# Emitting tile transposes one by one between the matmuls of a product, with two more idle products at the start

## The chip, the core and the metric

The kernel runs on one NeuronCore of a Trainium2 chip. A core has a matrix engine (TensorE, "PE" in the profile, with its weight loads shown apart as "PEld"), a vector engine (VectorE, "DVE"), a scalar engine (ScalarE, "ACT"), GpSimd ("POOL") and SyncE ("SP"), which here issues the DMAs. Each engine works through its own instructions in the order in which they were emitted; semaphores order the engines among each other. Matmuls read SBUF and write PSUM; ScalarE and VectorE read PSUM and write SBUF.

The metric is the device time of one execution in microseconds (us), the median of several runs.

## What is computed

One layer over 2048 positions of width 640, in float32, with no bias:

```
xn = layernorm(x)                                  # x: 2048 x 640
q, k, v = split(xn @ wqkv)                         # 32 heads of 20
s = softmax(q . k[pos - 2*w], w = 0..7) @ v[...]   # 8 keys, every second position back
s = s @ wo
h = (xn @ w_gate) * (xn @ w_up)                    # 640 -> 1536
g = silu(h @ w_down)                               # 1536 -> 640
out = x + s * g
```

All large products must keep float32's accuracy. The kernel gets it from the faster 32-bit matmul format fp32r: an operand is split into a high part (rounded by a ScalarE copy) and a low part (the rest, by a subtraction), and a product is the sum of high x high, high x low and low x high.

## The kernel before, in words

The 2048 positions are 16 tiles of 128. Everything is emitted by hand in one order (the tile framework is in its manual mode), so the order of the program text is the order on each engine.

- `mm3` (line 82) is a product: for KD = 5 slices of the inner dimension and three pairs of parts it emits 15 matmuls into one PSUM tile. `qkv(u, i)` (218) is one such product of 300 or 360 columns, followed by two ScalarE copies out of PSUM (226, 227). `gate_up(f, ch)` (312) is two of 512 columns (gate, then up), with ScalarE, VectorE or GpSimd taking the results. `out_proj(s)` (397) is two of 320 columns, each followed by a ScalarE copy (404).
- A tile must have its inner dimension on the partitions, so each tile is transposed on TensorE: five transposes of 128 x 128 against an identity matrix. `transposed` (191) does it: four go into one PSUM tile and one into a second, both of tag "q"; after each PSUM tile ScalarE copies out the high part (196) and VectorE subtracts for the low part (197). `trans(s)` (199) does it for an input tile, `trans_o(s)` (386) for a tile of the attention's output.
- PSUM tag "q" has four buffers. `qkv`, `out_proj`, the idle products and the transposes all take theirs from it. A buffer is free again when the engines that read it are done.
- `norm` (176) normalises tiles on VectorE, with one square root on ScalarE in its midst; `norm(12, 4)` works on the last four input tiles.

The head of the program (lines 556 to 607) is a list of calls: norms, weight splits, `trans(0)` to `trans(15)`, and the first `qkv` and `gate_up` products between them. TensorE's first work is a loop of three idle products against the identity (146), whose result nobody reads. In this list `trans(6)` stands between the two products of `gate_up(1, 0)` and `trans(11)` between those of `gate_up(1, 1)` (the argument `amid`); the others stand between whole calls.

Then, to about 556 us, the attention of 12 units runs on VectorE in portions (`advance`) while TensorE does the remaining `qkv` and `gate_up` products. At the end the attention's output comes back tile by tile (`load_o`, into buffers "wraw", "hs" and "t"), and a loop over s (678) calls `trans_o(s + 1)`, then `sum_wd` (VectorE sums of the down weights), then `out_proj(s)`, then `split_wd`. The last stage, after 645 us, is the down product in seven sub-products a pair of tiles, and the gating.

Of the kernel before, what the change touches and what calls it, by code (L numbers as in the profile page):

```python
# [11 lines left out]
F32 = mybir.dt.float32  # L12
F32R = mybir.dt.float32r
AF = mybir.ActivationFunctionType
# [5 lines left out]
P = 128  # L20
# [27 lines left out]
def kernel(  # L48
# [9 lines left out]
    nc = tc.nc  # L58
# [10 lines left out]
    def st(shape, tag, bufs, dt=F32):  # L69
        cnt[0] += 1  # L70
        return sb.tile(shape, dt, tag=tag, bufs=bufs, name=f"{tag}_{cnt[0]}")

    def pt(shape, tag, bufs):
        cnt[0] += 1
        return ps.tile(shape, F32, tag=tag, bufs=bufs, name=f"{tag}_{cnt[0]}")

    def split(eng, raw, hi, lo):

        nc.scalar.activation(hi, raw, AF.Copy)  # L79
        eng.tensor_sub(lo, raw, hi.bitcast(F32))  # L80

    def mm3(acc, pairs, first=True, last=True):

        pairs = list(pairs)
        runs = [(a[i], b[j]) for i, j in ((0, 0), (0, 1), (1, 0)) for a, b in pairs]
        for n, (a, b) in enumerate(runs):
            nc.tensor.matmul(acc, a, b, start=first and n == 0, stop=last and n == len(runs) - 1)  # L87


    wq_raw, wq = {}, {}  # L90

    def load_wq(g, parts):
        c3 = 3 * GROUPS[g] * DH
        wq_raw[g] = []
        for p in parts:
            t = st([P, p[-1] - p[0], c3], "wraw", 3)
            for k0, k1 in zip(p, p[1:]):
                nc.sync.dma_start(t[:, k0 - p[0]:k1 - p[0]], wqkv[g][:, k0:k1, :])
                wq_raw[g].append((k0, k1, t[:, k0 - p[0]:k1 - p[0]]))

    def split_wq(g, eng, ks=(0, KD)):
        c3 = 3 * GROUPS[g] * DH
        if g not in wq:
            wq[g] = st([P, KD, c3], "wqh", 1, F32R), st([P, KD, c3], "wql", 1, F32R)
        for k0, k1, t in wq_raw[g]:
            if ks[0] <= k0 < ks[1]:
                split(eng, t, wq[g][0][:, k0:k1], wq[g][1][:, k0:k1])
# [16 lines left out]
    def load_x(s, n, t, cuts=(0, D)):  # L124
        j = tile_column(s)
        for c0, c1 in zip(cuts, cuts[1:]):
            nc.sync.dma_start(t[:, :, c0:c1], xv[:, j:j + DIL * (n - 1) + 1:DIL, c0:c1])  # L127
        for i in range(n):
            xt[s + i] = t[:, i, :]
# [13 lines left out]
    load_x(15, 1, xb[:, 2:3])  # L143
    ident = st([P, P], "ident", 1)
    make_identity(nc, ident)
    for _ in range(3):
        nc.tensor.matmul(pt([P, 3, P], "q", 4), ident, ident.unsqueeze(1).to_broadcast([P, 3, P]), start=True,
                         stop=True)
    eps_t = st([P, 1], "eps", 1)
    nc.vector.memset(eps_t, EPS)  # L150

# [6 lines left out]
    def xT_tile(s):  # L158
        if s % TPC == 0:
            y = st([P, 2, KD, CH], "xc", NCH, F32R)  # L160
            xT.append((y[:, 0], y[:, 1]))
        hi, lo = xT[s // TPC]
        c = (s % TPC) * P
        return hi[:, :, c:c + P], lo[:, :, c:c + P]
# [24 lines left out]
                                    op0=ALU.subtract, op1=ALU.mult)  # L189

    def transposed(src, hi, lo):
        for k0, k1 in ((0, 4), (4, KD)):
            p = pt([P, k1 - k0, P], "q", 4)
            for k in range(k0, k1):
                nc.tensor.transpose(p[:, k - k0, :], src[:, k * P:(k + 1) * P], ident)  # L195
            nc.scalar.activation(hi[:, k0:k1, :], p, AF.Copy)  # L196
            nc.vector.tensor_sub(lo[:, k0:k1, :], p, hi[:, k0:k1, :].bitcast(F32))  # L197

    def trans(s):
        transposed(xt[s], *xT_tile(s))  # L200


    UN = [(g, r) for g in range(len(GROUPS)) for r in range(DIL)]
# [14 lines left out]
    def qkv(u, i):  # L218
        g, r = UN[u]
        c = GROUPS[g] * DH  # L220
        p = pt([P, 3 * c], "q", 4)
        hi, lo = xT[(r * NE + i) // TPC]
        t0 = (i % TPC) * P
        a, b = (hi[:, :, t0:t0 + P], lo[:, :, t0:t0 + P]), wq[g]
        mm3(p, [([t[:, k, :] for t in a], [t[:, k, :] for t in b]) for k in range(KD)])
        nc.scalar.activation(kv_t[u][:, :, W - 1 + i, :], p[:, c:].rearrange("p (a c) -> p a c", a=2), AF.Copy)  # L226
        nc.scalar.activation(q_t[u][:, i, :], p[:, :c], AF.Copy)
        for i0, i1 in ((1, 5), (5, NE)):
            if i == i1 - 1:
                for p0, p1 in ((0, 112), (112, 127)):  # L230
                    nc.sync.dma_start(kv_t[u][p0 + 1:p1 + 1, :, i0 - 1:i1 - 1, :],
                                      kv_t[u][p0:p1, :, W - 1 + i0:W - 1 + i1, :])
# [63 lines left out]
    def advance(budget):  # L296
        credit[0] += budget
        while running and credit[0] > 0:
            try:
                credit[0] -= next(running[0][1])  # L300
            except StopIteration:
                running.pop(0)
        if not running:
            credit[0] = 0
# [4 lines left out]
    def gate_up_half(f, ch, n, p, c=slice(0, CH)):  # L309
        mm3(p[:, c], [([t[:, k, n, :] for t in wf[f]], [t[:, k, c] for t in xT[ch]]) for k in range(KD)])  # L310

    def gate_up(f, ch, between=(), amid=(), part=None):
        if part is None:
            pp = [pt([P, CH], "g", 2), pt([P, CH], "u", 2)]
            c = slice(0, CH)
        else:
            pp, c = part, slice(CH // 2, CH)
        gate_up_half(f, ch, 0, pp[0], c)
        for act in amid:
            act()  # L320
        gs = st([P, CH], "gs", 2)
        nc.scalar.activation(gs, pp[0], AF.Copy)  # L322
        for act in between:
            act()
        share = (c.stop - c.start) / CH
        finish_piece()
        advance(PACE * 3.25 * share)
        gate_up_half(f, ch, 1, pp[1], c)

        def finish():  # L330
            hs = st([P, CH], "hs", 2)
            if running:
                nc.vector.tensor_mul(hs, pp[1], gs)  # L333
            else:
                nc.scalar.activation(hs, pp[1], AF.Copy)
                nc.gpsimd.tensor_mul(hs, hs, gs)  # L336
            nc.sync.dma_start(h_scr[ch * TPC:(ch + 1) * TPC, :, f, :].rearrange("t p c -> p t c"),
                              hs.rearrange("p (t c) -> p t c", c=P))

        unfinished.append(finish)  # L340
        if not running:
            finish_piece()
        advance(PACE * 3.25 * share)
# [3 lines left out]
    def finish_piece():  # L347

        while unfinished:
            unfinished.pop(0)()  # L350
# [37 lines left out]
    def trans_o(s):  # L388
        if s == NT - 2:
            oT[s] = st([P, KD, P], "hs", 2, F32R), st([P, KD, P], "hs", 2, F32R)  # L390
        else:
            tag, n = ("kv", 2) if s == 0 else ("wf", 4) if s < NT - 2 else ("t", 2)
            y = st([P, 2, KD, P], tag, n, F32R)
            oT[s] = y[:, 0], y[:, 1]
        transposed(o_t.pop(s), *oT[s])

    def out_proj(s):
        a = oT.pop(s)
        y = st([P, D], "gs", 2)
        for n in range(2):  # L400
            c = slice(n * HALF, (n + 1) * HALF)
            p = pt([P, HALF], "q", 4)
            mm3(p, [([t[:, k, :] for t in a], [t[:, c] for t in wo_s[k]]) for k in range(KD)])
            nc.scalar.activation(y[:, c], p, AF.Copy)
        nc.sync.dma_start(s_scr[s], y)
# [87 lines left out]
    bank, kept, g_t, sx_t = {}, {}, {}, {}  # L493
# [63 lines left out]
    mv1 = moments(1, 1)  # L557
    split_wq(0, nc.gpsimd, (0, 3))
    trans(0)
    split_wq(0, nc.gpsimd, (3, KD))  # L560
    load_x(13, 1, xa[:, 0:1])
    norm(1, 1, mv1)
    begin_unit(0)
    mv2 = moments(2, 2)
    qkv(0, 0)
    trans(1)
    split_wf(0, nc.gpsimd, range(KD + 1))
    norm(2, 2, mv2)
    qkv(0, 1)
    split_wf(1, nc.gpsimd, range(KD + 1))  # L570
    part0 = gate_up_first(0, 0)
    trans(2)
    trans(3)
    mask = st([1, NE, W], "mask", 1)
# [6 lines left out]
    gate_up(0, 0, part=part0)  # L581
    trans(4)
    trans(5)
    gate_up(1, 0, amid=(lambda: trans(6),))
    trans(7)
    norm(8, 4)
    load_wf(2)
    qkv(0, 4)
    qkv(0, 5)
    gate_up(0, 1)  # L590
    trans(8)
    qkv(0, 6)
    trans(9)
    norm(12, 4)
    qkv(0, 7)
    trans(10)
    gate_up(1, 1, amid=(lambda: trans(11),))
    begin_unit(1)
    for i in range(8):
        if i == 3:  # L600
            running.append((0, attention(0)))
        if i == 2:
            load_wq(1, ((0, 3), (3, 5)))
        qkv(1, i)
        if i < 4:
            trans(12 + i)
        advance(PACE * 1.9)
    running.append((1, attention(1)))
    split_wq(1, nc.gpsimd)
# [68 lines left out]
    for s in range(NT):  # L678
        k, part = divmod(s - 1, 2)
# [27 lines left out]
    for m in range(n_prod):  # L707
        n, j = divmod(m, 7)
# [52 lines left out]
```

## Time and profile before

| what | value |
|---|---|
| median of 3 runs | 803.85 us (803.69 to 804.44) |
| the profiled execution's own time | 803.25 us |
| its span, first to last instruction | 801.5 us |
| TensorE busy | 791.7 us, 99% |
| VectorE busy | 635.2 us, 79% |
| ScalarE busy | 236.7 us, 30% |
| GpSimd busy | 137.7 us, 17% |
| transposes (line 195) | 160: 80 of input tiles, 80 of attention tiles |

Rows of the profile name a line of the kernel, an engine, an operation and the tiles, "out<-in". A row of the view in order of time begins with the start and the length in us and ends with the number of instructions merged into it ("x5") and, in brackets, the idle time of the engine ahead of it and what ended that. Matmuls are pipelined and their ends are modelled, so the step from one start to the next tells more than a length; TensorE counts as busy while it merely holds a pipelined matmul. In the view of stretches each row gives, after the length, every engine's busy time, then the granted clock of TensorE (1.00 is full), the share of the DMA engines and GB/s.

### The profile page before, as it was taken

To read this page: it belongs to the slowest core of one execution; us is meant where nothing else is said; L and a number is where in the kernel's file an instruction comes from. 1 tells how busy PE (TensorE), PEld (TensorE's weight loads), DVE (VectorE), ACT (ScalarE), POOL (GpSimd) and SP (SyncE) were. 2 spreads that over 40 slices of the span, in tenths; PEclk is the share of its full clock that TensorE was granted. 3 is DMA by queue.
4 is the path that set the end of the run, shared out by engine and by line. 5 is a ranking of instruction groups with operands and counts; after the bars stand their busy time and mean duration, and the time that the engine had idled before them with its cause. 6 is when DMAs were issued, how large, how long until landed. Compare 5 with 4: busy or idle time off the path is not lost.

```text
span 801.5 us, 11434 instructions
## 1 busy us (share of the span) xinstructions
PE 791.7 (99%) x4564; PEld 721.5 (90%) x4564; DVE 635.2 (79%) x638; ACT 236.7 (30%) x560; POOL 137.7 (17%) x109
## 2 busy tenths in 40 slices
PE   8999999999999999999999999999999999999997
PEld 6889898898898898898989889888899999999997
DVE  7676899999999979997999999990144457878775
ACT  4323212121112111211121112102355554444442
POOL 5201210122012100500231001104266500000000
PEclk9999999999999999999999999999999999999999
DMA  9122012141122221313141222422867464565523
GB/s 318 63 80 89 28 61 79 51 121 48 49 88 86 87 70 60 116 39 97 49 137 42 68 72 78 129 61 75 214 191 206 139 251 136 201 224 185 178 99 132
DMA packets 68413, 90.07 MB, mean 112 GB/s; under 512 B 16952, under 2 KB 48776, under 8 KB 68360
## 3 DMA queue, kind: packets, MB, share of 16 engines
q1 hardware_dynamic: 68360, 89.34, 34.7%
q8 instruction: 36, 0.59, 0.3%
q14 instruction: 17, 0.14, 0.1%
HBM read 51.90 MB, written 28.31 MB: 100 GB/s over the span
## 4 chain that ended last, share of the span: by engine, by line
PE 96%; DMA 1%; POOL 1%; issue 1%; ACT 0%; DVE 0%; SPq 0%; POOLq 0%
PE q L87 35%; PE g L87 20%; PE u L87 20%; PE q L526 10%; PE u L526 5%; PE g L526 3%; PE q L195 2%; DMA wraw<-in_wqkv 1%; DMA hs<-o_scr 0%; POOL wf L80 0%; POOL wql L80 0%; ACT xc L196 0%; DVE q L512 0%; POOL hs L336 0%; SPq L127 0%
## 5 line engine op out<-in xcount | busy, mean ns | idle before, releaser
L87 PE MATMUL g<-xc,wf 128*128 128x512 f32 (+1 forms) x735 | 176.3, 391 | 0.1
L87 PE MATMUL u<-xc,wf 128*128 128x512 f32 (+1 forms) x735 | 176.1, 390 | 0.0
L87 PEld LDWEIGHTS u<-xc,wf 128*128 128x128 f32 x735 | 135.6, 187 | 32.2
L87 PE MATMUL q<-wqh,xc 128*128 128x300 f32 (+1 forms) x960 | 161.8, 311 | 2.1 <-ACT xc L196 1.6
L87 PEld LDWEIGHTS g<-xc,wf 128*128 128x128 f32 x735 | 135.2, 188 | 31.2 <-POOL wf L80 0.3
L87 PEld LDWEIGHTS q<-wqh,xc 128*128 128x128 f32 x960 | 146.8, 189 | 4.2 <-ACT xc L196 2.1
L258 DVE TENSOR_TENSOR t<-q,kv 128x1600 f32<-128x1600 f32 (+1 forms) x48 | 101.7, 2119 | 9.1 <-DMA kv<-kv 9.1
L279 DVE TENSOR_TENSOR t<-e,kv 128x1600 f32<-128x1600 f32 (+1 forms) x48 | 97.6, 2053 | 1.1
L261 DVE TENSOR_REDUCE lg<-t 128x80 f32<-128x1600 f32 (+1 forms) x48 | 92.6, 1930 | 1.2
L322 ACT ACTIVATE gs<-g 128x512 f32<-128x512 f32 x48 | 28.8, 599 | 207.5 <-PE g L87 198.8
L80 POOL TENSOR_TENSOR wf<-wraw,wf 128x256 fp32r<-128x256 f32 (+2 forms) x22 | 44.8, 2053 | 249.1 <-ACT wf L79 249.1
L87 PE MATMUL q<-wql,xc 128*128 128x300 f32 (+1 forms) x480 | 87.0, 311 | 0.2 <-POOL wql L80 0.2
L287 DVE TENSOR_TENSOR t<-t,t 128x1600 f32<-128x1600 f32 (+1 forms) x36 | 78.0, 2166 | 1.1
L226 ACT ACTIVATE kv<-q 128x200 f32<-128x200 f32 (+1 forms) x96 | 33.4, 348 | 145.9 <-PE q L87 145.9
L87 PEld LDWEIGHTS q<-wql,xc 128*128 128x128 f32 x480 | 74.8, 189 | 0.6 <-POOL wql L80 0.5
L526 PE MATMUL q<-xc,wf 128*128 128x320 f32 x432 | 67.3, 309 | 0.0
L526 PEld LDWEIGHTS q<-xc,wf 128*128 128x128 f32 x432 | 64.3, 188 | 0.0
L80 POOL TENSOR_TENSOR wql<-wraw,wqh 128x300 fp32r<-128x300 f32 (+4 forms) x15 | 33.4, 2254 | 147.8 <-ACT wqh L79 147.8
L197 DVE TENSOR_TENSOR wf<-q,wf 128x512 fp32r<-128x512 f32 (+1 forms) x26 | 11.5, 486 | 41.7 <-ACT wf L196 41.7
L87 PE MATMUL q<-wf,wf 128*128 128x320 f32 x156 | 36.8, 317 | 0.0
L197 DVE TENSOR_TENSOR xc<-q,xc 128x512 fp32r<-128x512 f32 (+1 forms) x32 | 13.9, 484 | 20.7 <-ACT xc L196 20.7
L333 DVE TENSOR_TENSOR hs<-u,gs 128x512 f32<-128x512 f32 x39 | 26.6, 683 | 0.8 <-issue 0.8
(144 smaller groups left out, 900.9 us busy)
## 6 DMA issues: line engine op xcount, KB each, us to landing
h_scr<-hs SPq DMA_DIRECT2D x48, 256.0 KB, 2.3
wraw<-in_wgu SPq DMA_DIRECT2D x12, 640.0 KB, 4.5
t<-h_scr SPq DMA_DIRECT2D x8, 768.0 KB, 7.4
s_scr<-gs SPq DMA_DIRECT2D x16, 320.0 KB, 2.3
hs<-s_scr SPq DMA_DIRECT2D x16, 320.0 KB, 3.7
gs<-in_x SPq DMA_DIRECT2D x16, 320.0 KB, 4.2
out<-q SPq DMA_DIRECT2D x15, 320.0 KB, 2.4
wraw<-h_scr SPq DMA_DIRECT2D x12, 384.0 KB, 6.1
```

Source lines behind the costliest of these rows:

```text
L80: eng.tensor_sub(lo, raw, hi.bitcast(F32))
L87: nc.tensor.matmul(acc, a, b, start=first and n == 0, stop=last and n == len(runs) - 1)
L195: nc.tensor.transpose(p[:, k - k0, :], src[:, k * P:(k + 1) * P], ident)
L197: nc.vector.tensor_sub(lo[:, k0:k1, :], p, hi[:, k0:k1, :].bitcast(F32))
L226: nc.scalar.activation(kv_t[u][:, :, W - 1 + i, :], p[:, c:].rearrange("p (a c) -> p a c", a=2), AF.Copy)
L258: nc.vector.tensor_mul(t, q.rearrange("p i c -> p (i c)").unsqueeze(1).to_broadcast([P, 2, NE * c]), places(0, j))
L261: nc.vector.tensor_reduce(out=lg[:, :, j:j + 2].rearrange("p n a -> p a n"), in_=heads(t), op=ALU.add, axis=AX.X)
L279: nc.vector.tensor_mul(heads(t), pw, heads(places(1, j)))
L287: nc.vector.tensor_add(acc, acc, t)
L322: nc.scalar.activation(gs, pp[0], AF.Copy)
L333: nc.vector.tensor_mul(hs, pp[1], gs)
L526: nc.tensor.matmul(p, y[:, i, k], wd_t[name][k][:, l], start=new and r == 0, stop=r == len(runs) - 1, skip_group_check=True)
```

## The change

Transposes are no longer emitted where `trans` or `trans_o` is called. They are put into a list, `single`, as five small functions a tile, and `mm3` emits one of them after every second matmul (seven places in a product of 15). The PSUM tile is taken, and the ScalarE copy and the VectorE subtraction are emitted, when the first and the last transpose of their bank are emitted. A call of `trans(s)` without `mixed` still empties the list at once; so does `trans_o(0)`. Input tiles 0 to 5 and attention tile 0 therefore stay in groups; input tiles 6 to 15 and attention tiles 1 to 15 go between matmuls: 6 and 7 in `gate_up(1, 0)`, 8 in `qkv(0, 6)`, 9 in `qkv(0, 7)`, 10 and 11 in `gate_up(1, 1)`, 12 to 15 in `qkv(1, 0)` to `qkv(1, 3)`, attention tile s + 1 in the first half of `out_proj(s)`. The call of `norm(12, 4)` stays between `trans(9)` and `qkv(0, 7)`.

The idle product becomes a function; four are emitted at the start in place of three, and one more after `trans(0)`.

```
--- before.py
+++ after.py
@@ mm3
         for n, (a, b) in enumerate(runs):
             nc.tensor.matmul(acc, a, b, start=first and n == 0, stop=last and n == len(runs) - 1)
+            if n % 2 and single:
+                single.pop(0)()
+
+    single = []
+
+    def singles():
+        while single:
+            single.pop(0)()
@@ head
-    for _ in range(3):
+    def idle_product():
+
         nc.tensor.matmul(pt([P, 3, P], "q", 4), ident, ident.unsqueeze(1).to_broadcast([P, 3, P]), start=True,
                          stop=True)
+
+    for _ in range(4):
+        idle_product()
@@ transposed
     def transposed(src, hi, lo):
+
+        bank = {}
+
+        def one(k, k0, k1):
+            if k == k0:
+                bank[k0] = pt([P, k1 - k0, P], "q", 4)
+            p = bank[k0]
+            nc.tensor.transpose(p[:, k - k0, :], src[:, k * P:(k + 1) * P], ident)
+            if k == k1 - 1:
+                nc.scalar.activation(hi[:, k0:k1, :], p, AF.Copy)
+                nc.vector.tensor_sub(lo[:, k0:k1, :], p, hi[:, k0:k1, :].bitcast(F32))
+
         for k0, k1 in ((0, 4), (4, KD)):
-            p = pt([P, k1 - k0, P], "q", 4)
             for k in range(k0, k1):
-                nc.tensor.transpose(p[:, k - k0, :], src[:, k * P:(k + 1) * P], ident)
-            nc.scalar.activation(hi[:, k0:k1, :], p, AF.Copy)
-            nc.vector.tensor_sub(lo[:, k0:k1, :], p, hi[:, k0:k1, :].bitcast(F32))
-
-    def trans(s):
+                single.append(lambda k=k, k0=k0, k1=k1: one(k, k0, k1))
+
+    def trans(s, mixed=False):
         transposed(xt[s], *xT_tile(s))
+        if not mixed:
+            singles()
@@ trans_o
         transposed(o_t.pop(s), *oT[s])
+        if s == 0:
+            singles()
@@ the list of calls
     trans(0)
+    idle_product()
...
     trans(4)
     trans(5)
-    gate_up(1, 0, amid=(lambda: trans(6),))
-    trans(7)
+    trans(6, True)
+    trans(7, True)
+    gate_up(1, 0)
     norm(8, 4)
     load_wf(2)
     qkv(0, 4)
     qkv(0, 5)
     gate_up(0, 1)
-    trans(8)
+    trans(8, True)
     qkv(0, 6)
-    trans(9)
+    trans(9, True)
     norm(12, 4)
     qkv(0, 7)
-    trans(10)
-    gate_up(1, 1, amid=(lambda: trans(11),))
+    trans(10, True)
+    trans(11, True)
+    gate_up(1, 1)
...
     for i in range(8):
...
+        if i < 4:
+            trans(12 + i, True)
         qkv(1, i)
-        if i < 4:
-            trans(12 + i)
         advance(PACE * 1.9)
```

## The prediction

> **What bounds the kernel now.** I read the page first (span, busy shares), then busy time by stretch, then what TensorE waits for, then the groups of instructions, and last the order of time around each place that the change touches.
>
> ```profile
> span 801.5 us, 11434 instructions
> PE 791.7 (99%) x4564; PEld 721.5 (90%) x4564; DVE 635.2 (79%) x638; ACT 236.7 (30%) x560; POOL 137.7 (17%) x109
> 75.00:556.00 481.00, 481.00 (x2520) 422.72 (x2519) 440.76 (x305) 95.91 (x250) 72.83 (x27) 1.00 0.24 74
> PE q L87 <- ACT xc L196: 1.6, 2, 1.1
> PE q L195 <- DVE t L188: 0.7, 1, 0.7
> PE q L195 <- DMA hs<-o_scr: 0.4, 1, 0.4
> ```
>
> TensorE (PE) is busy 791.7 of 801.5 us, and between 75 and 556 us all 481.00 of 481.00 us (the columns are the length of the stretch, then PE and PE's weight loads). So PE's own queue is the path: whatever is added to it, or makes it wait, before 645 us is paid in full, and nothing later takes it up. The waits that the profile lists for PE are short and lie in the head and at one tile of the attention output. No listed wait belongs to tiles 4 to 15 of the input. So emitting their transposes elsewhere can only gain if a transpose itself gets cheaper.
>
> **Part 1: what a transpose costs in a group and alone.** Each tile has five transposes, L195. These rows are the chain that ended last (start, length, what; x15 products of 512 columns among it), the durations of one line (minimum, median, maximum in ns) and PE in order of time:
>
> ```profile
> 595.37 4.42 PE q L87 x30
> 599.79 0.55 PE q L195 x5
> 600.34 4.42 PE q L87 x30
> 544.01 3.50 PE u L87 x15
> L195 PE MATMUL q<-ident,xc x40: 270/272/273, 29.5 to 59.6; 128*128 128x128 f32 x40
> 27.79 1.92 PE L87 MATMUL u<-xc,wf 128*128 128x256 f32 x15
> 29.54 1.25 PE L195 MATMUL q<-ident,xc 128*128 128x128 f32 x10
> ```
>
> A group of five takes 0.55 us, 0.110 each. Ten in a row last 1.25 us from the first start to the last end, and one lasts 0.272 us, so the step from transpose to transpose is (1.25 - 0.27) / 9 = 0.109 us. Four such steps leave 0.55 - 0.436 = 0.114 us for the step from the last transpose to the next product. A transpose that stands alone between two matmuls has only that second kind of step; the matmul ahead of it keeps its own pace. Alone it therefore costs 0.114 against 0.110 in the group. Fifty transposes in the head (tiles 6 to 15) and 75 at the end (attention tiles 1 to 15) are moved: 125 x 0.005 = **+0.6 us**. Ends: 0, if the step is the same, and 125 x 0.009 = +1.1, if the last step is 0.118; below nothing stands the rival "hidden transposes".
>
> **Part 2: tile 6 in gate_up(1, 0).** The transposes write PSUM tiles of tag "q", of which there are four; a tile takes two, and each is free only after ScalarE (L196) and then VectorE (L197) have read it.
>
> ```profile
> 30.55 3.74 PE L87 MATMUL g<-xc,wf 128*128 128x512 f32 x15
> 30.86 1.68 DVE L197 TENSOR_TENSOR xc<-q,xc 128x512 fp32r<-128x512 f32 x4 [0.45 <-ACT xc L196]
> L197 DVE TENSOR_TENSOR xc<-q,xc x32: 278/460/693, 8.1 to 75.0; 128x512 fp32r<-128x512 f32 x16, 128x128 fp32r<-128x128 f32 x16
> ```
>
> Tiles 4 and 5 are still transposed at once and fill all four. Before, tile 6 came after 15 gate matmuls; now its first transpose comes after two. Fifteen take 3.50 us, 0.233 each, and the first really follows the group of ten, at 29.54 + 10 x 0.110 = 30.64 (the row's 30.55 is its early start). So tile 6 is reached at about 30.64 + 0.47 = 31.1 us, while VectorE finishes the first of the four subtractions, a long one of 0.69, at 30.86 + 0.69 = 31.55. Nothing else of PE can pass: **+0.5 us** (0.3 to 0.6).
>
> **Part 3: tiles 8 to 11 and norm(12, 4). This is the largest term.** Before, tile 9's evictions were emitted ahead of norm(12, 4). Now tile 9's transposes, and with them its ScalarE copies and VectorE subtractions, are emitted inside qkv(0, 7), behind norm(12, 4); VectorE works in that order.
>
> ```profile
> 49.84 0.71 PE L195 MATMUL q<-ident,xc 128*128 128x128 f32 x5
> 51.16 0.89 DVE L197 TENSOR_TENSOR xc<-q,xc 128x512 fp32r<-128x512 f32 x2 [3.16 <-ACT xc L196]
> 52.46 0.71 PE L195 MATMUL q<-ident,xc 128*128 128x128 f32 x5
> 52.66 0.34 ACT L226 ACTIVATE kv<-q 128x200 f32<-128x200 f32 x1 [1.36 <-PE q L87]
> 55.08 0.71 PE L195 MATMUL q<-ident,xc 128*128 128x128 f32 x5
> 53.73 0.89 DVE L197 TENSOR_TENSOR xc<-q,xc 128x512 fp32r<-128x512 f32 x2 [1.68 <-ACT xc L196]
> 54.54 0.87 DVE L172 BATCH_NORM_STATS2 stats<-o 128x6 f32<-128x320 f32 x2
> 58.66 0.30 ACT L180 ACTIVATE rstd<-mv,eps 128x4 f32<-128x4 f32 x1 [4.80 <-DVE mv L173]
> 62.10 1.68 DVE L197 TENSOR_TENSOR xc<-q,xc 128x512 fp32r<-128x512 f32 x4
> ```
>
> The reader sees norm(12, 4) hold VectorE from 54.54 until the next subtraction at 62.10, 7.56 us, and ScalarE stand at its square root (L180) for 4.80 us. Call the start of qkv(0, 6) zero (49.84 before). 52.46 to 55.08 is one tile and one qkv: 2.62 us, 15 matmuls at 0.138 and a group. In the changed order tile 8's fourth transpose starts after 8 matmuls and 3 transposes, at 1.45. By the rows (fourth transpose at 49.84 + 3 x 0.109 = 50.17, subtractions from 51.16 to 52.05, the next work 0.81 after such a start: as tile 9's at 53.73 and 54.54) its VectorE work is over near 1.45 + 0.99 + 0.81 = 3.25, call it 3.2, and norm(12, 4) runs from 3.2 to 10.76. Tile 9's first subtraction ends at 10.76 + 0.69 = 11.45. PE meanwhile would reach the third transpose group as follows: two qkv with five single transposes each, 2 x 2.64 = 5.28, then twelve gate matmuls and five transposes, 12 x 0.233 + 5 x 0.112 = 3.36, which is tile 11's first transpose at 8.65. By then all four PSUM tiles are taken: two by tile 9, two by tile 10, none of them subtracted. It waits for tile 9's first, to about 11.5: **+2.85 us**. On the way it may already lose part of this (0.2 to 0.4 at tile 9, which needs tile 8's PSUM; 0.5 at tile 10's second group, since qkv(0, 7)'s result waits behind the square root on ScalarE), but the end at 11.5 is set by VectorE, so these are in the 2.85. Ends: 2.3 if VectorE is ready 0.5 earlier, 3.4 if tile 10's second group takes the late tile. Behind the waiting transpose stands the rest of PE's program.
>
> **Part 4: tiles 12 to 15 in qkv(1, 0) to (1, 3).** Same PSUM tag: qkv's result and two transposed banks of one tile, then the next qkv's result, four in all. The next tile's first transpose comes two matmuls into the next qkv, 2.64 + 0.28 = 2.92 after the start of the one before; the first bank is released at 1.45 + 0.99 + 0.69 = 3.13 (0.99 from its fourth transpose to its subtraction, as in part 3), or, if the bank of the qkv result is taken, at about 3.3: its first copy starts at 52.66, 2.82 after zero, lasts 0.34, and a second follows. That is 0.2 to 0.4 a tile, three times: **+0.9 us** (0.4 to 1.2). No attention work is on VectorE yet.
>
> **Part 5: attention tile 1.** Here the old order waits.
>
> ```profile
> 599.63 0.71 PE L195 MATMUL q<-ident,t 128*128 128x128 f32 x5
> 565.46 3.67 PE L87 MATMUL u<-xc,wf 128*128 128x512 f32 x15
> 569.49 1.01 PE L195 MATMUL q<-ident,hs 128*128 128x128 f32 x5 [0.36 <-DMA hs<-o_scr]
> 570.50 4.42 PE q L87 x30
> ```
>
> PE is free at 565.46 + 15 x 0.233 = 568.96, starts the tile at 569.49 as its load lands in pieces, and the products follow at 570.50 rather than 568.96 + 0.70 = 569.66 (0.70 is from 599.63, where an undisturbed group starts, to 600.34 in part 1). That is 0.84 late. Now two products go first (0.29), the first transpose waits about 0.24 and the others find their pieces: **-0.6 us** (-0.8 to -0.3).
>
> The other tiles of that stage are covered: transposes end ten matmuls into out_proj(s), and the result is read 20 matmuls x 0.147 = 2.9 us later, low half 10 matmuls later still. What moves ahead of their subtraction on VectorE is sum_wd:
>
> ```profile
> 587.33 0.89 DVE L197 TENSOR_TENSOR wf<-q,wf 128x512 fp32r<-128x512 f32 x2 [3.19 <-ACT wf L196]
> 588.13 0.57 DVE L435 TENSOR_TENSOR lg<-wraw 128x320 f32<-128x320 f32 x1
> 588.80 1.00 DVE L436 TENSOR_TENSOR lg<-wraw,lg 128x320 f32<-128x320 f32 x1
> ```
>
> Even if its 1.67 us lie wholly ahead, the subtraction ends near 589.9, and the low half is read from about 591.2. Without that cover each tile would cost the overshoot. SyncE's loads into the "t" buffer (s = 3, 6, 9) now wait for a transpose about 2 us later, with out_proj's stores and the weight loads behind them; tile 8 is wanted four periods of 4.97 us later, so this costs nothing.
>
> **Part 6: the head.** Start and length on PE and the row of VectorE that tile 1 waits for, then two stretches (length, PE busy, weight loads, DVE, ACT, POOL, granted clock):
>
> ```profile
> 1.37 4.21 PE L147 MATMUL q<-ident 128*128 128x384 f32 x6 [1.37 <-POOL ident masks.py:199]
> 6.28 0.76 PE L195 MATMUL q<-ident,t 128*128 128x128 f32 x5 [0.70 <-DVE t L188]
> 8.10 1.26 PE L87 MATMUL q<-wqh,xc 128*128 128x300 f32 x5 [1.06 <-ACT xc L196]
> 10.95 1.12 DVE L188 TENSOR_SCALAR t<-t,mv,rstd 128x640 f32<-128x640 f32 x1
> 12.23 0.92 PE L195 MATMUL q<-ident,t 128*128 128x128 f32 x5
> 5.83:9.24 3.41, 1.90 (x11) 1.44 (x12) 2.47 (x8) 2.88 (x8) 2.70 (x4) 1.00 1.03 374
> 9.25:12.66 3.41, 3.25 (x14) 2.79 (x13) 3.24 (x8) 0.19 (x1) 2.46 (x3) 0.50 0.94 312
> ```
>
> PE was busy 1.90 of the first stretch and got half the clock in the next. An idle product is two instructions of about 0.64 us; the fourth starts near 5.4, gets the full clock from 5.83 and ends near 6.28, where tile 0 starts: nothing, or +0.4 at half clock. The fifth fits between 7.0 and 8.10. With the clock kept, tile 1, which cannot start before 10.95 + 1.12 = 12.07, ends 0.3 earlier (five transposes last 0.71 at full clock, 0.92 here, and start 0.16 sooner), and ScalarE, POOL and PE behind it follow: **-0.3 us**. Ends: -0.4, and +1.0 if the now thinner stretch from 9.25 loses the clock for the next.
>
> **Sum.** 0.6 + 0.5 + 2.85 + 0.9 - 0.6 - 0.3 = +3.95 us on the profiled execution's 803.25 us, 807.2; it stands 0.6 under the median shown, so I forecast **807.8 us** for the median.
>
> **The rivals.**
> - *Hidden transposes (faster).* If a lone transpose cost only the stream of its 128 columns, at the rate of the 256-column products (29.54 - 27.79 = 1.75 us for 15, 0.117 each), it would take 0.058, and 125 x 0.052 = 6.5 us would go: 803.85 + 3.35 - 6.5 = 800.7. It decides from 0.083 us a transpose downwards (0.110 - 3.35 / 125). Against it: the step to the next product, 0.114, is measured already and a lone transpose consists of it. The Trainium skill, "TensorE: Matmul & The Clock Gate", section "Part 2: What happens when you issue a matmul", says that the next tile's weights load while this one's matmul runs, and gives N/2.4 + 2.5 ns between isolated matmuls; an estimate by that page is 56 ns a transpose, which makes 800.4. The trace has 0.109 between transposes whose weight loads may overlap just so, which disagrees.
> - *The stall also costs the clock.* A wait of over 2 us leaves PE less busy in a stretch than the 1.90 us above; 3.41 us at half clock would add 1.7: 809.5. For it: the 0.50 row. Against: the wait may be split over two stretches.
> - *No stall in part 3* (VectorE's work or the PSUM tiles fall otherwise): 807.8 - 2.85 = 804.95, inside what can be told from no change, about 0.2% or 1.6 us.
>
> **How the numbers follow.** Forecast 0.52, own range 806.5 to 808.9 from the bounds above; lost clock 0.30; no stall 0.08; hidden 0.08; the head at its +1.0 end 0.02. Leaving out hidden and no stall, the range is 805.6 to 810.2. Faster 0.08, within 0.2% 0.06, slower 0.86.
>
> **What would show it.** PE in the changed profile: a wait of about 2 us before a transpose in gate_up(1, 1), released by VectorE's L197, right after norm(12, 4); half-microsecond waits at tiles 6, 9 and 13 to 15; matmul, transpose, matmul in the last stage with a period of 4.97 to 5.01 us a tile; the clock at 1.00 from 9.25 to 12.66. A period of 4.7 us would mean that transposes are hidden, and no VectorE release of PE near 60 us that the largest term is wrong.

## The result and the profile after

The changed kernel takes 808.4 us in the median of 6 runs (807.18 to 808.59) against 803.77 us before (803.35 to 804.44): a ratio of 1.0055 with a 95% interval of 1.0042 to 1.0068, so slower by half a per cent. The profiled execution took 808.55 us.

The page's first lines, two rows of the busy time by stretch (length, PE, weight loads, DVE, ACT, POOL, granted clock, DMA) and, last, the first of these two stretches in the profile before:

```profile
span 806.8 us, 11447 instructions
PE 794.7 (99%) x4568; PEld 720.8 (89%) x4568; DVE 634.2 (79%) x638; ACT 238.2 (30%) x560; POOL 136.8 (17%) x109
30.00:75.00 45.00, 42.29 (x235) 35.12 (x234) 22.99 (x65) 14.45 (x41) 6.33 (x5) 0.96 0.24 72
75.00:556.00 481.00, 480.95 (x2536) 423.57 (x2535) 442.71 (x307) 96.26 (x254) 69.20 (x25) 1.00 0.24 74
...
30.00:75.00 45.00, 45.00 (x278) 40.71 (x277) 24.64 (x68) 16.14 (x49) 6.38 (x5) 1.00 0.24 72
```

The span grew by 5.3 us and TensorE (PE) is still at 99%. The middle of the program is as full as before, so it gave nothing back. The loss lies between 30 and 75 us, where PE was busy throughout, is now idle for 2.7 us and runs a part of the time at less than the full clock. The waits of PE, and of its weight loads between 28 and 82 us, name the cause (who waited for whom: total, times, longest):

```profile
PE q L211 <- DVE xc L214: 2.3, 2, 2.0
PEld q L211 <- DVE xc L214: 4.4, 6, 2.4
PEld q L211 <- ACT q L250: 0.6, 1, 0.6
```

L211 is the transpose, L214 the subtraction on VectorE that gives a PSUM tile free (L195 and L197 before). Six times a transpose waited for it, where before none of tiles 4 to 15 did. The largest one, in order of time:

```profile
50.15 0.44 PE L87 MATMUL q<-wqh,xc 128*128 128x300 f32 x2
53.32 0.88 DVE L184 BATCH_NORM_STATS2 stats<-o 128x6 f32<-128x320 f32 x2
57.46 0.30 ACT L192 ACTIVATE rstd<-mv,eps 128x4 f32<-128x4 f32 x1 [4.01 <-DVE mv L185]
58.83 0.33 PE L211 MATMUL q<-ident,xc 128*128 128x128 f32 x1 [0.20 <-ACT q L250]
60.90 1.68 DVE L214 TENSOR_TENSOR xc<-q,xc 128x512 fp32r<-128x512 f32 x4
61.64 0.33 PE L211 MATMUL q<-ident,xc 128*128 128x128 f32 x1 [2.01 <-DVE xc L214]
```

qkv(0, 6) starts at 50.15. norm(12, 4) holds VectorE from 53.32 to 60.90, with ScalarE standing at its square root (L192) until 57.46. Tile 10's second bank waits until 58.83 for ScalarE, which copies qkv(0, 7)'s result out of the buffer only behind that square root. Tile 11's first transpose waits for VectorE until 61.64, 11.49 us after the start of qkv(0, 6). What the stall did to the clock, in stretches of 3.41 us, the length for which the clock stood at 0.50 (62.80 to 66.22 us):

```profile
59.39:62.80 3.41, 1.40 (x8) 0.98 (x7) 3.19 (x8) 0.09 (x1) 0.00 (x0) 1.00 0.31 89
62.81:66.21 3.40, 3.40 (x11) 2.43 (x11) 0.70 (x2) 1.47 (x3) 0.00 (x0) 0.50 0.02 5
66.22:69.63 3.41, 3.41 (x22) 3.05 (x21) 0.27 (x1) 0.60 (x1) 0.69 (x1) 1.00 0.00 0
```

PE was busy 1.40 of 3.41 us in the stretch with the wait, and the next stretch ran at 0.50: 11 matmuls and transposes in it where the one after has 22.

The smaller waits, as the chain shows them (start, length, what; "issue" is time in which the engine waited for nothing that the profile shows): tile 6, then tile 13, which is one of three alike.

```profile
30.58 0.70 DVE xc L214
31.28 0.04 issue
31.33 0.33 PE q L211
...
69.75 0.61 ACT xc L213
70.36 0.02 issue
70.38 0.70 DVE xc L214
71.09 0.04 issue
71.13 0.33 PE q L211
...
74.04 0.33 PE q L211
```

In each the transpose starts 0.05 us after the subtraction that it needs. From tile 13 to tile 14 PE takes 74.04 - 71.13 = 2.91 us, where before 2.62 passed from tile to tile. The attention stage and the head:

```profile
596.90 3.24 PE q L87 x22
600.14 0.11 PE q L211
600.25 0.30 PE q L87 x2
601.88 3.24 PE q L87 x22
...
571.08 3.67 PE L87 MATMUL u<-xc,wf 128*128 128x512 f32 x15
574.58 0.47 PE L87 MATMUL q<-wf,kv 128*128 128x320 f32 x2
575.07 0.30 PE L211 MATMUL q<-ident,hs 128*128 128x128 f32 x1
575.50 0.27 PE L211 MATMUL q<-ident,hs 128*128 128x128 f32 x1
...
12.13 0.74 PE L211 MATMUL q<-ident,t 128*128 128x128 f32 x5 [0.49 <-PE q L87]
13.45 0.96 PE L87 MATMUL q<-wqh,xc 128*128 128x300 f32 x5 [0.58 <-ACT xc L213]
9.25:12.66 3.41, 2.24 (x14) 1.57 (x12) 3.27 (x7) 0.48 (x2) 2.43 (x3) 1.00 0.90 328
```

A lone transpose takes 0.11 us of the chain, as one in a group did; the period of a tile is 601.88 - 596.90 = 4.98 us, against 4.97. At attention tile 1 the first products follow the last gate_up without a gap (574.58), and its first transpose is 0.2 us late where the old group lost 0.84. In the head the clock is at 1.00 from 9.25 to 12.66 us, where the kernel before had 0.50, and the products after tile 1 start at 13.45 instead of 13.73.

### The profile page after: what moved, and what is told of

Same layout as the page of the kernel before. It is cut to its first block, busy times and chain, and to the rows that moved or that the text cites. A ratio compares the mean times of both kernels' runs of the same rounds, so it can differ in the third digit from the quotient of the medians.

```text
span 806.8 us, 11447 instructions
## 1 busy us (share of the span) xinstructions
PE 794.7 (99%) x4568; PEld 720.8 (89%) x4568; DVE 634.2 (79%) x638; ACT 238.2 (30%) x560; POOL 136.8 (17%) x109
## 4 chain that ended last, share of the span: by engine, by line
PE 95%; DVE 2%; ACT 1%; POOL 1%; issue 1%; DMA 0%; SPq 0%
PE q L87 34%; PE u L87 21%; PE g L87 20%; PE q L551 10%; PE u L551 5%; PE g L551 3%; PE q L211 2%; DVE xc L214 1%; ACT xc L213 1%; DMA wraw<-in_wqkv 0%; POOL wf L80 0%; DVE stats L184 0%; POOL wql L80 0%; DVE q L537 0%; DVE t L200 0%
## 5 line engine op out<-in xcount | busy, mean ns | idle before, releaser
L87 PE MATMUL g<-xc,wf 128*128 128x512 f32 (+1 forms) x735 | 178.2, 392 | 0.1
L87 PE MATMUL u<-xc,wf 128*128 128x512 f32 (+1 forms) x735 | 178.2, 393 | 0.0
L214 DVE TENSOR_TENSOR xc<-q,xc 128x512 fp32r<-128x512 f32 (+1 forms) x32 | 14.0, 484 | 25.4 <-ACT xc L213 25.3
L214 DVE TENSOR_TENSOR wf<-q,wf 128x512 fp32r<-128x512 f32 (+1 forms) x26 | 11.5, 482 | 23.5 <-ACT wf L213 23.5
```

## The experiments

Every kernel was run in five rounds against the kernel before; 803.68 us is its median in the first four comparisons and 804.02 us in the last three.

**Only the idle products.** The kernel before, with

```
-    for _ in range(3):
+    for _ in range(4):
         idle_product()
...
     trans(0)
+    idle_product()
```

> The kernel before with only the idle products changed (four at the start, one after tile 0's transposes). Theory: they keep the clock at 1.00 from 9.25 us on, tile 1 is done 0.3 us earlier and the rest follows, 803.8 - 0.3 = 803.5 us. Rival: part of the changed kernel's 4.6 us comes from them (a late tile 0, or a cold stretch later in the head), 804.2 us or more.

Measured: 803.46 us, ratio 0.9996 (0.9987 to 1.0005). The rival that the idle products cost something falls; that they gain is not shown either, since the interval includes 1. In the profile the head is 0.32 us ahead of the kernel before from qkv(0, 1) on, with the clock at 1.00. Then a load takes it back: PE in order of time at attention tile 2.

```profile
574.39 0.60 PE L199 MATMUL q<-ident,t 128*128 128x128 f32 x4
575.37 0.30 PE L199 MATMUL q<-ident,t 128*128 128x128 f32 x1 [0.38 <-DMA t<-o_scr]
```

The fifth transpose waits for a DMA, as none of tile 2's did in the profile before.

**Only the attention tiles between matmuls.** The kernel before with the list of single transposes, emptied at once by every `trans(s)`:

```
     def trans(s):
         transposed(xt[s], *xT_tile(s))
+        singles()
```

> The kernel before with only the attention tiles 1 to 15 transposed one by one in out_proj. Theory: a lone transpose costs 0.114 us against 0.110 in a group, 75 x 0.005 = +0.4, and tile 1 no longer holds TensorE for its load, -0.8: 803.8 - 0.4 = 803.4 us, and the period of a tile grows from 4.97 to 4.99. Rival, hidden transposes: 75 x 0.052 = 3.9 us are gained, 799.1 us, period 4.71.

Measured: 802.81 us, ratio 0.9987 (0.9978 to 0.9996): faster than the kernel before by 0.87 us. The theory said 0.4; the interval is 0.3 to 1.8 us, so it does not tell the two apart. Transposes are not hidden; that rival wanted 799.1.

**Tile 9 as a group.** The changed kernel with

```
-    trans(9, True)
+    trans(9)
     norm(12, 4)
```

> The changed kernel with tile 9 transposed as a group at its call, so that its subtractions stand ahead of norm(12, 4) on VectorE again; tiles 6 to 8 and 10 to 15 stay between matmuls. Theory: the wait of 2.9 us around tile 11 goes, and with it the 1.5 us of the stretch at half clock: 808.4 - 4.4 = 804.0 us, clock at 1.00 after 60 us. Rival, the lone transposes themselves are the loss: 808.3 us. Rival, only the wait goes and the clock falls for another reason: 805.5 us.

Measured: 804.32 us, ratio 1.0006 (0.9997 to 1.0014). One call moves the time by 4.1 us. The lone transposes are not the loss, since 45 of the 50 input transposes still stand alone here. VectorE in order of time, the wait that is left for the weight loads between 28 and 82 us, and the stretch that had run at half clock:

```profile
54.04 0.89 DVE L214 TENSOR_TENSOR xc<-q,xc 128x512 fp32r<-128x512 f32 x2 [0.64 <-ACT xc L213]
54.84 0.88 DVE L184 BATCH_NORM_STATS2 stats<-o 128x6 f32<-128x320 f32 x2
...
PEld q L211 <- DVE xc L214: 1.7, 4, 0.8
...
62.81:66.21 3.40, 3.40 (x24) 3.21 (x23) 1.39 (x5) 1.32 (x3) 1.54 (x2) 1.00 0.03 5
```

Tile 9's subtractions now go ahead of the norm, four of the six waits are left (tiles 6 and 13 to 15), and the clock stays at 1.00. The rival by which only the wait goes, 805.5 us, falls too.

**PE kept busy in the wait.** The changed kernel, with three idle products into the free buffer of tag "g" just ahead of tile 11's first transpose:

```
     trans(11, True)
+    tile11 = single[-5]
+    def busy_then_tile11():
+        p = pt([P, 3, P], "g", 2)
+        for _ in range(3):
+            nc.tensor.matmul(p, ident, ident.unsqueeze(1).to_broadcast([P, 3, P]), start=True, stop=True)
+        tile11()
+    single[-5] = busy_then_tile11
```

> The changed kernel with three more idle products (about 0.64 us each, 1.9 in all) just ahead of tile 11's first transpose, where TensorE waits 2.0 us for VectorE. Theory: the wait ends at the same time, about 61.6 us, but TensorE is busy in it, the clock stays at 1.00 and the 1.5 us of the half clock are saved: 806.9 us. Rival, the half clock is no matter of the wait, or costs nothing: 808.4 us. Rival, the products come on top of the wait: 810.3 us.

Measured: 807.03 us in 5 runs (806.78 to 807.25), ratio 1.0037 (1.0025 to 1.005). Work that nobody reads makes the kernel 1.4 us faster. The mean granted clock is 1.000 in all five runs; in the changed kernel it is 0.997 or 0.998 in five of six.

```profile
59.56 2.10 PE L630 MATMUL g<-ident 128*128 128x384 f32 x6
61.73 0.33 PE L211 MATMUL q<-ident,xc 128*128 128x128 f32 x1
...
57.46:60.87 3.41, 3.18 (x15) 2.00 (x14) 3.04 (x11) 2.02 (x7) 0.00 (x0) 1.00 0.22 62
60.87:64.28 3.41, 3.33 (x16) 2.18 (x15) 1.80 (x5) 0.82 (x2) 0.00 (x0) 1.00 0.09 27
64.28:67.70 3.42, 3.42 (x21) 2.98 (x20) 0.89 (x2) 1.23 (x3) 0.25 (x1) 1.00 0.02 5
```

Tile 11 starts as late as before (61.73 against 61.64), so the wait itself is not shortened; what is saved is the stretch at half clock. Wait and clock are two separate losses.

**No waits for PSUM.** Tile 9 as above, and tiles 6, 7 and 12 to 15 back in their old places:

```
-    trans(6, True)
-    trans(7, True)
-    gate_up(1, 0)
+    gate_up(1, 0, amid=(lambda: trans(6),))
+    trans(7)
...
-        if i < 4:
-            trans(12 + i, True)
         qkv(1, i)
+        if i < 4:
+            trans(12 + i)
```

> The changed kernel with tiles 6, 7, 9 and 12 to 15 transposed as before and only 8, 10 and 11 (and the attention tiles) between matmuls; idle products as changed. Theory: beside the 4.1 us that tile 9 as a group took away, the wait at tile 6 (0.6) and the three at tiles 13 to 15 (0.3 each) go: 804.3 - 1.5 = 802.8 us. Rival, these losses are the price of lone transposes and not waits for PSUM: 35 transposes fewer alone change 0.2 us at most, 804.1 us.

Measured: 802.78 us, ratio 0.9987 (0.9978 to 0.9996). The 1.5 us go, as they must if the loss at these tiles is waiting; the rival, 804.1, falls.

**The two harmless parts together.** The kernel before with both of the first two edits.

> The kernel before with the two harmless parts of the change: attention tiles between matmuls and the idle products; no input tile is moved. Theory: the gains add, 802.8 - 0.3 = 802.5 us, faster than both kernels. Rival, the head's gain depends on where the clock's stretches fall and does not show in the median: 802.8 us.

Measured: 802.44 us (802.32 to 802.74), ratio 0.9982 (0.9974 to 0.9991): the lowest median of the study, faster than both of the case. Whether the idle products have a part in it is not shown: the interval overlaps that of the attention tiles alone (0.9978 to 0.9996). Its runs lie within 0.42 us of each other, those of the kernel before in the same comparison between 803.07 and 805.32.

**Attention tile 1 alone.** The same, but all attention tiles other than 1 stay in groups:

```
-        if s == 0:
+        if s != 1:
             singles()
```

> The kernel before with the idle products and with attention tile 1 alone between matmuls, the one tile that waits for its load. Theory: the lone transposes of the other 14 tiles cost 0.012 us a tile more than groups (the period's growth), so leaving them as groups gains 0.2 us: 802.3 us. Rival, mixing the other tiles also covers late loads that some executions have, and without it the time is higher: 802.8 us or more.

Measured: 803.5 us, ratio 0.9994 (0.9985 to 1.0002). The expectation of 802.3 missed and its rival was right. PE at attention tile 2:

```profile
573.68 0.49 PE L211 MATMUL q<-ident,t 128*128 128x128 f32 x3
574.49 0.33 PE L211 MATMUL q<-ident,t 128*128 128x128 f32 x1 [0.32 <-DMA t<-o_scr]
575.20 0.30 PE L211 MATMUL q<-ident,t 128*128 128x128 f32 x1 [0.38 <-DMA t<-o_scr]
575.25 0.54 PE L87 MATMUL q<-wf,wf 128*128 128x320 f32 x2
```

Tile 2's load lands piece by piece until 575.20, and as a group the transposes now meet it too early: from the group's start to the next product 1.57 us pass, where in the profile before 0.51 passed at this tile. These 1.06 us are also what this kernel's median lies above the one with all attention tiles mixed. What mixing gains at this place is cover for two late loads, not for one.

## Why the prediction was right, and where not

Going by the starts of the same matmuls in the profiles before and after, the prediction's steps against what they cost:

| step | predicted | measured |
|---|---|---|
| 1, lone transposes (125) | +0.6 | about +0.2: the period grew by 0.013 us a tile, 15 tiles; the input tiles' share is in the rows below |
| 2, tile 6 | +0.5 | +0.6 |
| 3, tiles 8 to 11 | +2.85, tile 11 at 11.5 after qkv(0, 6) | tile 11 at 11.49; (62.62 - 50.15) - (59.60 - 49.84) = 2.71 to the up product of gate_up(1, 1), with three transposes still to come: 2.71 + 3 x 0.11 = +3.04 |
| 4, tiles 13 to 15 | +0.9 | 3 x (2.91 - 2.62) = +0.87 |
| 5, attention tile 1 | -0.6 | -0.6 (0.84 late before, 0.2 now) |
| 6, head | -0.3 | 13.45 - 13.73 = -0.28 |
| rival, half clock after the stall | +1.7, left out of the sum | the up product and those three transposes: (68.01 - 62.62) - (63.17 - 59.60) - 3 x 0.11 = +1.5 |

The up product and the product behind it, before and then after:

```profile
59.60 3.74 PE L87 MATMUL u<-xc,wf 128*128 128x512 f32 x15
63.17 0.86 PE L87 MATMUL q<-wqh,xc 128*128 128x300 f32 x5
...
62.62 0.89 PE L87 MATMUL u<-xc,wf 128*128 128x512 f32 x2
68.01 0.44 PE L87 MATMUL q<-wqh,xc 128*128 128x300 f32 x2
```

The steps without the clock make 0.2 + 0.6 + 3.04 + 0.87 - 0.6 - 0.28 = 3.83 us, where the sum had 3.95; with 1.5 for the clock they make 5.3, and the two profiled executions differ by 808.55 - 803.25 = 5.3.

**The mechanism held.** The order on VectorE (tile 9's subtractions behind norm(12, 4)) and four PSUM buffers set the loss. The one-call edit at tile 9, the return of tiles 6 and 12 to 15, and the waits by name show it. What more buffers would do was not run. Of the signs that the prediction named, the wait before tile 11, the clock in the head and the period came as said; the waits at tiles 9 and 13 to 15 were about 0.3 us and not half a microsecond.

**What was mis-sized: the chance of the half clock.** "The stall also costs the clock" was given 0.30 and the forecast 0.52. By the granted clock the profiled execution lost it, and the times say that most did: 807.18 us is the one run of six that stands apart, 1.2 us below the median; its mean clock was 0.999 where the five others had 0.997 or 0.998, and it lies among the runs with idle products in the wait. So the median of 808.4 is not the forecast's case but the rival's, with a price of about 1.5 instead of 1.7, on a sum that was right to 0.1 us because the lone transposes were 0.4 too high and tiles 6 and 8 to 11 together 0.3 too low. That the forecast of 807.8 lies only 0.6 us from the median is in part luck. It left the clock's 1.5 us out, and the medians differ by 808.4 - 803.77 = 4.63 us, 0.7 less than the two profiled executions. Where that 0.7 lies is not shown; a gain from the mixed attention tiles above the 0.6 of step 5, which the second experiment's median of 0.87 allows, would be a part of it. The argument against the rival, that the wait may fall into two stretches, counted for too much.

**Hidden transposes** are out: a lone one takes 0.11 us of the chain. The step that spoke against it, that the price of transpose-to-product was measured already, was the right reading.

**Not separated:** whether the two added idle products keep the clock in the head, and which of them. In the second experiment, which has neither, the head of the profiled execution was 0.26 us ahead of the kernel before all the same, so that the 0.3 us also depends on where the clock's stretches fall in an execution. Under what busy time in a stretch the clock is lost is narrowed, not settled. In stretches counted in steps of 3.41 us from a change of the clock, 1.40 us (changed kernel) and 1.90 us (kernel before) of 3.41 were followed by half clock. This one of the changed kernel, with 2.34 us busy, was not; its clock stays at 1.00 from there to 62.80 us:

```profile
11.60:15.01 3.41, 2.34 (x17) 2.09 (x17) 3.34 (x10) 2.69 (x10) 1.14 (x3) 1.00 1.00 365
```

## What to carry to other kernels

Before work is moved between the instructions of a busy engine, look at what its results are queued behind on the engines that read them: moved past one call, tile 9's 0.9 us of subtractions came behind 7.6 us of VectorE work, and four PSUM buffers turned that into a wait of 2 us on the engine that bounds the kernel. Spreading work only pays where something late is covered by it (here the loads of two attention tiles, 0.87 us in the second experiment) and does not pay where the engine was full and nothing waited. And a wait on TensorE is to be priced with the clock that it may cost after it.

## What was not expected of the hardware

The prediction gave the half clock only 0.30. A single wait of 2.01 us was enough for half a clock in the next 3.41 us, and filling it with idle products gave back 1.4 us. The Trainium skill, "TensorE: Matmul & The Clock Gate", section "Why this matters for your kernels", asks for no PE-idle gaps over about 3 us between bursts of matmuls; here PE idled 2.0 us, with 1.40 busy in the stretch, and the measurement decides: a shorter gap suffices.
